# Block-summary rows ahead of the local rows, and a new order table, in an attention layer with two feed-forward layers

## The chip, the cores and the metric

The kernel runs on one core of a Trainium2 chip. The metric is the device time of one execution in microseconds (us). The core's engines are named as the profile names them: PE does matrix multiplications (PEld is the loading of their stationary operand), DVE and ACT work on rows of 128 partitions, POOL is a third such engine, SP issues the transfers between the memory outside the core (HBM) and its own (SBUF); 16 DMA engines carry them out. PE writes into PSUM. Each engine runs its instructions strictly in the order in which they were written, and waits where an operand is not there yet.

## What is computed

Two batches of 768 rows, eight heads of 64. Every row attends to the rows within 15 places of it, and to 24 summaries of the whole sequence: the maximum of k and the mean of v over each block of 32 rows. Its result, 1536 rows of 512 values, goes through two feed-forward layers 512 to 2048 to 512 with different gates. All of it is in float32.

```
k_sum = k.reshape(B, H, nb, block, D).max(axis=3)
v_sum = v.reshape(B, H, nb, block, D).mean(axis=3)
scores_l = scale * (q @ k.T), masked to |i - j| < 16
scores_s = scale * (q @ k_sum.T) + log(block)
a = softmax(concatenate([scores_l, scores_s]))
x = a @ concatenate([v, v_sum])
x = gate(x @ w_in) @ w_out         # h / (1 + exp(-1.702 h))
x = gate(x @ moe2_w_in) @ moe2_w_out  # h * cos(h)
```

## The kernel before

**Attention.** The 1536 rows are twelve units of 128. A unit is two halves (g) of 64 rows, and a half sees 96 local rows (`GW`) and the 24 summaries (`NB`), 120 columns in all (`GC`), the local ones first. Scores come out with rows on partitions and 120 columns free (L407); DVE adds the mask and takes the maximum in one instruction (L414); ACT takes the exponential and its sum (L421); DVE divides (L424 to L430); PE transposes (L456 for the early units, L522 for the others), ACT copies the result to SBUF (L466, L525), and PE multiplies it with the values (L436). There the 120 columns are partitions: the window of values in `vw` or `vy` has its 96 local rows on partitions 0 to 95 and the 24 summary rows on 96 to 119. The local rows are loaded from `vwin` (`load_v`, L330, one transfer of 96 rows of 4 KB); the summary rows are written by `put_vsum`, once by ACT from PSUM (L360) and three times by POOL (L358).

**The summaries.** `ksum_of` (L368) takes block maxima on DVE. `vsum_mm` (L381) gets the block means of v from six matmuls of a 0 or 1/32 selector, sliced out of the tile `blk` 120 columns wide, of which 24 hold something.

**The first four units** (batch 0) are done in eight early pieces, n = 0 to 7: four heads of one unit each, heads 0 to 3 of the four units first. Each piece is: scores on PE, L414 on DVE, four exponentials on ACT, sums and norm on DVE, transposes on PE, copy on ACT, values on PE, and then the feed-forward input `xh`: its rounded part on ACT (L494), the rest on DVE (L495). Feed-forward steps for the first 512 rows can start when the `xh` of a head group of all four units is there. The eight other units are done between feed-forward steps.

**Feed-forward.** Per layer and per 512 rows there are 16 steps; each has 12 matmuls of 128x512 for h (L704), the gate on ACT and DVE, and 12 for the output (L830): 96 steps, 2304 matmuls. The weights come in 32 transfers of 1 MB (`w_load`, L611: chunk 0, 1, 2, ...). A chunk is converted before use (`convert`): L623 on ACT ("scale"), L629 ("low") and L633 ("join") on DVE, then twice L650 on ACT (high part) and L654 on DVE (low part). Chunk 0 holds what the first two h steps need.

**What sets the order.** Nothing is issued as it is written. Every piece of work is an `Op` with an engine, a planned duration and its predecessors; `order_of` lays them out engine by engine in planned time, by the length of the way behind each plus a number from the table `BONUS`, and the instructions are then written in that order (L260 is the line of nearly all transfers, since `dma` records them). The planned durations and the table only decide the order. All loads go through one queue, SP's, and the first 17 are chained in one written order (`wanted`): kf, qf, mask, identity, blk, vf, the window v of unit 0, weight chunk 0, the windows of units 1 to 3, weight chunk 1.

Of the kernel before, what the change touches and what calls it, by code (L numbers as in the profile page):

```python
# [55 lines left out]
    "at": 15248.9, "early at": 4670.1, "early exp": -10174.0, "early load v": 7117.2, "early load w": -9997.1,  # L56
    "early norm": -26626.0, "early pv": -19642.9, "early s": -8955.9, "early sum": -21555.4, "early t": 28276.7,
    "early ttr": -8099.7, "early w hi": -32048.9, "early w join": 3108.9, "early w lo": -20901.2,
    "early w low": 14427.2, "early w scale": 2678.5, "early xc": 272.9, "early xl": -7387.2, "evac": 19328.8,
    "exp": -10511.6, "g hi": 6093.0, "g lo": 3352.9, "gate": 20097.5, "h": -2002.2, "ksum": -8099.2,  # L60
    "load blk": -15675.4, "load ident": -7247.9, "load k": 9987.0, "load k1": -2486.3, "load kf0": -3352.8,
    "load kf1": 4225.3, "load mask": 42433.3, "load q": -7043.4, "load qf0": -12789.8, "load qf1": -4538.6,
    "load v": -6728.3, "load vf": 10952.8, "load vf1": 226.0, "load w": -6499.3, "norm": 3592.2, "out": -2000.2,
    "put ksum": 23793.3, "put vsum": -23481.1, "put vsum pool": -2105.8, "pv": 1324.1, "pv s": -3914.3,
    "s": -10696.2, "store": -2998.8, "sum": -22560.9, "sum vf1": 1824.3, "t": 10815.7, "ttr": -15482.4,
    "vsb": 3823.5, "vsum": 12059.7, "vsum1": -840.6, "w hi": 5478.0, "w join": -4468.7, "w lo": -3558.6,
    "w low": 6921.0, "w scale": 7315.3, "x hi": -12587.8, "x lo": -7344.2, "xc": -4143.9,
# [108 lines left out]
def order_of(ops):  # L176
# [24 lines left out]
    start, end = listed(ops, START, before, behind, {o: way[o] + BONUS.get(o.kind, 0.0) for o in ops}, True)  # L201
# [8 lines left out]
def local_global_attention_two_ffn(  # L210
# [64 lines left out]
    vsb = ex[1][0:GC, 1024:1024 + DM]  # L275
    blk = ex[1][:, 1536:1800]
# [49 lines left out]
    d_blk = dma("load blk", 0.37, blk, blkc)  # L326
    d_id = dma("load ident", 0.2, ident, identc)

    def load_v(i, dst, *deps):
        return dma(("early " if i < UT else "") + "load v", 1.6, dst[0:GW].rearrange("p g d -> p (g d)"), vwin[i], *deps)  # L330

    def load_k(i, *deps):
        b, j = divmod(i, NTILE)

        def fn():
            for g in range(2):
                c = 128 * j + 64 * g
                nc.sync.dma_start(out=kw[:, :, g, 0:GW], in_=kT[b, :, :, c:c + GW].rearrange("h p s -> p h s"))

        return op("load k", "DMA", 2.2, fn, *deps)  # L340

    def load_q(i, *deps):
        b, j = divmod(i, NTILE)
        return dma("load q", 1.1, qw, qT[b, :, :, 128 * j:128 * j + 128].rearrange("h p s -> p h s"), *deps)

    def put_ksum(b, hf, *deps):
# [3 lines left out]
            lambda: nc.gpsimd.tensor_copy(out=kw[:, 2 * hf:2 * hf + 2, :, GW:GC], in_=src.to_broadcast([128, 2, 2, NB])), *deps  # L350
# [772 lines left out]
```

## Time and profile before

| | |
|---|---|
| median of 3 runs | 590.74 us (590.04 to 593.53) |
| span of the profiled execution | 590.6 us |
| PE busy | 579.7 us, 98% |
| DVE busy | 400.2 us, 68% |
| ACT busy | 296.0 us, 50% |
| POOL busy | 15.9 us, 3% |
| moved by DMA | 55.06 MB, 93 GB/s over the span |

A busy PE in this table is not a PE at its peak. Shares over the whole span also hide that the first 40 us are a stage of another kind than the rest, so the rows below are mostly from there.

### The profile page before, as it was taken

What the parts mean: (1) busy time and instruction counts of PE and PEld (TensorE: products, weight loads), DVE (VectorE), ACT (ScalarE), POOL (GpSimd) and SP (SyncE); (2) the same over time, 40 slices, a digit from 0 to 9 for tenths busy, and PEclk for the clock granted to TensorE, in tenths of its full rate; (3) what the DMA queues carried; (4) which work ended last, traced back from release to release, by engine and by line L of the source; (5) the groups of instructions that cost most, each with busy time, mean ns of one, the idle gap of its engine ahead of it and who ended that gap; (6) DMA issues with size and microseconds to landing.
All of it is one profiled execution on the core that took longest, in us unless ns stands there. A gap on an engine that the chain in (4) does not pass through costs nothing.

```text
span 590.6 us, 8597 instructions
## 1 busy us (share of the span) xinstructions
PE 579.7 (98%) x3319; PEld 474.8 (80%) x3319; DVE 400.2 (68%) x810; ACT 296.0 (50%) x607; POOL 15.9 (3%) x19
## 2 busy tenths in 40 slices
PE   7899999999999999999999999999999999999997
PEld 5478888888888888888888888888888888888886
DVE  5689998965242436578878866667666667765664
ACT  5688678855153344465667533335433334333333
POOL 0101400000000000000000000000000000000000
PEclk8899999999999999999999999999999999999999
DMA  9978867733021116145550000000100000100001
GB/s 313 268 237 294 304 205 249 245 107 108 1 72 33 39 28 214 61 154 181 188 202 0 2 1 1 0 1 0 72 1 1 0 2 0 72 0 2 0 1 71
DMA packets 24200, 55.06 MB, mean 93 GB/s; under 512 B 9824, under 2 KB 15072, under 8 KB 20064
## 3 DMA queue, kind: packets, MB, share of 16 engines
q1 hardware_dynamic: 24016, 54.39, 28.3%
q8 instruction: 26, 0.43, 0.3%
q14 instruction: 14, 0.11, 0.1%
q10 hardware_dynamic: 144, 0.13, 0.1%
HBM read 51.37 MB, written 3.15 MB: 92 GB/s over the span
## 4 chain that ended last, share of the span: by engine, by line
PE 94%; DMA 3%; ACT 1%; SPq 0%; issue 0%; DVE 0%; ACTq 0%
PE h_ps L704 45%; PE acc L830 44%; DMA raw<-in_w_dram 2%; PE x_ps L436 2%; PE s_ps L407 1%; PE t_ps L522 1%; DMA kf<-in_kT_dram 1%; SPq L260 0%; PE t_ps L456 0%; ACT at_early L466 0%; ACT ex L421 0%; ACT wc L623 0%; PE vs_ps L381 0%; ACT xh L494 0%; ACT w L650 0%
## 5 line engine op out<-in xcount | busy, mean ns | idle before, releaser
L704 PE MATMUL h_ps<-xh,w 128*128 128x512 f32 x1152 | 291.8, 391 | 0.0
L830 PE MATMUL acc<-g,w 128*128 128x512 f32 x1155 | 290.4, 390 | 0.0
L704 PEld LDWEIGHTS h_ps<-xh,w 128*128 128x128 f32 x1152 | 215.5, 188 | 45.5 <-issue 0.3
L830 PEld LDWEIGHTS acc<-g,w 128*128 128x128 f32 x1155 | 216.1, 188 | 44.7 <-issue 0.5
L760 ACT CAST g<-gt 128x512 fp32r<-128x512 f32 x96 | 59.7, 622 | 91.5 <-PE acc L830 83.1
L764 DVE TENSOR_TENSOR g<-gt,g 128x512 fp32r<-128x512 f32 x96 | 66.1, 690 | 41.2 <-ACT g L760 40.9
L752 ACT ACTIVATE gt<-gt,half_pi 128x512 f32<-128x512 f32 x48 | 34.7, 723 | 64.1 <-DVE gt L748 64.0
L732 DVE SCALAR_TENSOR_TENSOR gt<-gt,h_ps 128x512 f32<-128x512 f32 x48 | 32.8, 684 | 28.8 <-ACT gt L726 28.8
L756 DVE TENSOR_TENSOR gt<-gt,h_ps 128x512 f32<-128x512 f32 x48 | 33.0, 688 | 26.8 <-ACT gt L752 26.8
L633 DVE SCALAR_TENSOR_TENSOR wc<-wc,raw 128x1024 uint32<-128x1024 uint32 x32 | 41.2, 1289 | 12.7 <-ACT wc L623 12.6
L728 ACT ACTIVATE gt<-h_ps 128x512 f32<-128x512 f32 x48 | 28.6, 597 | 35.4 <-PE h_ps L704 35.4
L726 ACT ACTIVATE gt<-h_ps 128x512 f32<-128x512 f32 x48 | 28.5, 595 | 34.1 <-PE h_ps L704 33.8
L654 DVE TENSOR_TENSOR w<-wc,w 128x512 fp32r<-128x512 f32 x64 | 45.3, 716 | 0.0
L623 ACT ACTIVATE wc<-raw 128x1024 f32<-128x1024 f32 x32 | 36.8, 1150 | 12.3 <-DVE w L654 7.3
L650 ACT CAST w<-wc 128x512 fp32r<-128x512 f32 x64 | 38.4, 618 | 4.4 <-DVE wc L633 4.2
L736 DVE TENSOR_SCALAR gt<-gt 128x512 f32<-128x512 f32 x48 | 20.5, 426 | 29.6 <-ACT gt L728 29.5
L740 DVE SCALAR_TENSOR_TENSOR r<-gt,h_ps 128x512 f32<-128x512 f32 x48 | 33.4, 696 | 1.6
L744 DVE SCALAR_TENSOR_TENSOR gt<-gt,r 128x512 f32<-128x512 f32 x48 | 32.9, 686 | 1.4
L629 DVE TENSOR_SCALAR raw<-raw 128x1024 uint32<-128x1024 uint32 x32 | 22.7, 709 | 5.7 <-DMA raw<-in_w_dram 5.7
L748 DVE TENSOR_SCALAR gt<-gt 128x512 f32<-128x512 f32 x48 | 20.4, 424 | 0.9
L414 DVE CUSTOM_DVE_ANT_0 room<-s_ps,mask_sb 128x120 f32<-128x120 f32 x32 | 6.8, 279 | 15.2 <-PE s_ps L407 15.2
L421 ACT ACTIVATE ex<-ex 128x120 f32<-128x120 f32 x32 | 12.2, 383 | 6.3 <-DVE ex L414 6.3
(74 smaller groups left out, 289.3 us busy)
## 6 DMA issues: line engine op xcount, KB each, us to landing
raw<-in_w_dram SPq DMA_DIRECT2D x32, 1024.0 KB, 4.8
win<-in_vwin_dram SPq DMA_DIRECT2D x9, 384.0 KB, 5.3
win<-in_kT_dram SPq DMA_DIRECT2D x16, 192.0 KB, 4.5
out_dram<-xf SPq DMA_DIRECT2D x11, 256.0 KB, 2.0
win<-in_qT_dram SPq DMA_DIRECT2D x8, 256.0 KB, 5.5
kf<-in_kT_dram SPq DMA_DIRECT2D x4, 400.0 KB, 5.4
k<-in_kT_dram SPq DMA_DIRECT2D x4, 400.0 KB, 8.1
vf<-in_v_dram SPq DMA_DIRECT2D x3, 512.0 KB, 8.5
```

The source lines that it names most:

```text
L623: nc.scalar.activation(out=t.bitcast(FP32), in_=raws[m][:, :, 1].bitcast(FP32), func=ACTF.Prelu, scale=REBIAS, alpha=SIGN)
L633: nc.vector.scalar_tensor_tensor(out=t, in0=t, scalar=3, in1=raws[m][:, :, 0], op0=ALU.logical_shift_left, op1=ALU.bitwise_or)
L650: nc.scalar.copy(out=w[:, 0, :], in_=mids[m][:, 512 * a:512 * (a + 1)].bitcast(FP32))
L654: nc.vector.tensor_tensor(out=w[:, 1, :], in0=mids[m][:, 512 * a:512 * (a + 1)].bitcast(FP32), in1=w[:, 0, :].bitcast(FP32), op=ALU.subtract,)
L704: nc.tensor.matmul(out=hs[i], lhsT=w[:, a, c], rhs=x[:, b, :], start=(k == 0 and n == 0), stop=(k == KD - 1 and n == 2),)
L740: nc.vector.scalar_tensor_tensor(out=r, in0=gts[i], scalar=-C1, in1=hs[i], op0=ALU.mult, op1=ALU.add)
L744: nc.vector.scalar_tensor_tensor(out=gt, in0=gt, scalar=-C2, in1=rs[0], op0=ALU.mult, op1=ALU.add)
L752: nc.scalar.activation(out=gt, in_=gt, func=ACTF.Sin, bias=half_pi)
L756: nc.vector.tensor_tensor(out=gt, in0=gt, in1=hs[i], op=ALU.mult)
L760: nc.scalar.copy(out=g[:, 0, :], in_=gts[i])
L764: nc.vector.tensor_tensor(out=g[:, 1, :], in0=gts[i], in1=g[:, 0, :].bitcast(FP32), op=ALU.subtract)
L830: nc.tensor.matmul(out=accs[d][:, c], lhsT=w[:, a, 128 * d:128 * (d + 1)], rhs=g[:, b, c], start=(f == 0 and n == 0), stop=(f == NF - 1 an ...
```

## The change

The 120 columns of a unit change places: the 24 summaries come first, the 96 local rows behind them. In the free dimension (k windows, mask, scores) this is another slice of the same tile. In the partition dimension the value windows now have summaries on partitions 0 to 23 and local rows on 24 to 119. The selector slices of `blk` shrink from 120 to 24 columns, the tile from 264 to 68 columns, and the block means come out on partitions 0 to 23. The planned durations of most transfers are lowered, and the table `BONUS` gets other values and one more entry for many single operations (`"at#4"` is the fifth of its kind). `order_of` adds both.

```diff
 BONUS = {
-    "at": 15248.9, "early at": 4670.1, "early exp": -10174.0, "early load v": 7117.2, "early load w": -9997.1,
...
+    "at": -196105.0, "at#0": -6600.5, "at#1": 28.6, "at#10": 32.2, "at#12": -1.8, "at#13": -7258.6, "at#14": -4925.8,
...
-    start, end = listed(ops, START, before, behind, {o: way[o] + BONUS.get(o.kind, 0.0) for o in ops}, True)
+    made, urgency = {}, {}
+    for o in ops:
+        n = made[o.kind] = made.get(o.kind, -1) + 1
+        urgency[o] = way[o] + BONUS.get(o.kind, 0.0) + BONUS.get(f"{o.kind}#{n}", 0.0)
+    start, end = listed(ops, START, before, behind, urgency, True)
...
-    vsb = ex[1][0:GC, 1024:1024 + DM]
-    blk = ex[1][:, 1536:1800]
+    vsb = ex[1][0:NB, 1024:1024 + DM]
+    blk = ex[1][:, 1536:1604]
...
-        return dma(("early " if i < UT else "") + "load v", 1.6, dst[0:GW].rearrange("p g d -> p (g d)"), vwin[i], *deps)
+        return dma(("early " if i < UT else "") + "load v", 1.1, dst[NB:GC].rearrange("p g d -> p (g d)"), vwin[i], *deps)
...
-                nc.sync.dma_start(out=kw[:, :, g, 0:GW], in_=kT[b, :, :, c:c + GW].rearrange("h p s -> p h s"))
...
-        return op("load k", "DMA", 2.2, fn, *deps)
+                nc.sync.dma_start(out=kw[:, :, g, NB:GC], in_=kT[b, :, :, c:c + GW].rearrange("h p s -> p h s"))
...
+        return op("load k", "DMA", 1.8, fn, *deps)
...
-            src = (vw[GW:GC, 0, :] if eng == "POOL" else vs()[GW:GC, :]).rearrange("p (o c) -> p o c", o=1)
+            src = (vw[0:NB, 0, :] if eng == "POOL" else vs()[0:NB, :]).rearrange("p (o c) -> p o c", o=1)
...
-                nc.gpsimd.tensor_copy(out=dst[GW:GC], in_=src)
+                nc.gpsimd.tensor_copy(out=dst[0:NB], in_=src)
...
-                nc.scalar.copy(out=dst[GW:GC], in_=src)
+                nc.scalar.copy(out=dst[0:NB], in_=src)
...
-                    out=ps[0][0:GC, :], lhsT=sel, rhs=t, start=(a == 0), stop=(a == len(parts) - 1)
+                    out=ps[0][0:NB, :], lhsT=sel, rhs=t, start=(a == 0), stop=(a == len(parts) - 1)
...
-        o = op(("early " if m < 2 else "") + "load w", "DMA", 3.3, fn)
+        o = op(("early " if m < 2 else "") + "load w", "DMA", 2.65, fn)
...
-            mask[m, rows, 0:GW] = np.where(ok, 0.0, -8.0e9)[rows]
-            mask[m, rows, GW:] = 8.0 * np.log(float(BLK))
-    blk = np.zeros((128, 264), np.float32)
+            mask[m, rows, NB:] = np.where(ok, 0.0, -8.0e9)[rows]
+            mask[m, rows, 0:NB] = 8.0 * np.log(float(BLK))
+    blk = np.zeros((128, 68), np.float32)
```

What the table moves is seen in the written order of the engines. The first 15 transfers keep their order. Two places differ that matter for the text below; line numbers of the changed kernel are 71 higher there.

**ACT, early part, before.** `ex` holds the early pieces' probabilities (L421 is the exponential, four to a piece), `at_early<-t_ps` is the copy behind the transposes, `wc<-raw` the scale of a weight chunk, `win<-vs_ps` the copy of the block means, `xh<-x_ps` the feed-forward input. These rows follow the start-up of ACT:

```order
L421 ACTIVATE ex<-ex 128x120 x24
L466 COPY at_early<-t_ps 120x512 x2
L623 ACTIVATE wc<-raw 128x1024
L466 COPY at_early<-t_ps 120x512
L360 COPY win<-vs_ps 24x1024
L466 COPY at_early<-t_ps 120x512
L421 ACTIVATE ex<-ex 128x120 x4
L466 COPY at_early<-t_ps 120x512
L494 CAST xh<-x_ps 128x2x128 x3
L466 COPY at_early<-t_ps 120x512
L421 ACTIVATE ex<-ex 128x120 x4
L466 COPY at_early<-t_ps 120x512
```

**ACT, the same place in the change**, up to shortly ahead of the third scale (L694), in two pieces that follow each other; L721 (`w<-wc`) is the high part of a weight half:

```order
L492 ACTIVATE ex<-ex 128x120 x20
L537 COPY at_early<-t_ps 120x512
L492 ACTIVATE ex<-ex 128x120 x4
L694 ACTIVATE wc<-raw 128x1024
L537 COPY at_early<-t_ps 120x512
L492 ACTIVATE ex<-ex 128x120 x4
L537 COPY at_early<-t_ps 120x512
L431 COPY win<-vs_ps 24x1024
L537 COPY at_early<-t_ps 120x512
L694 ACTIVATE wc<-raw 128x1024
L565 CAST xh<-x_ps 128x2x128
```

and on:

```order
L537 COPY at_early<-t_ps 120x512
L492 ACTIVATE ex<-ex 128x120 x4
L565 CAST xh<-x_ps 128x2x128
L537 COPY at_early<-t_ps 120x512
L565 CAST xh<-x_ps 128x2x128
L721 CAST w<-wc 128x512
L537 COPY at_early<-t_ps 120x512
L721 CAST w<-wc 128x512
L565 CAST xh<-x_ps 128x2x128 x2
L721 CAST w<-wc 128x512
L565 CAST xh<-x_ps 128x2x128
```

Behind the last row come a copy, a cast of weights, the scale of chunk 2 and the last two casts to `xh`. What moved: the scale of chunk 0 stands behind 24 of the 32 exponentials in both. The scale of chunk 1 stood behind everything of the eight pieces but the last two casts to `xh`; it now stands ahead of all eight casts, the last four copies, the last piece's exponentials, and the high parts of chunk 0 as well.

**PE, start of the feed-forward part, before** (`x_ps<-at_early` are the values of a piece, 8 matmuls; `t_ps<-ident,ex` its transposes; `h_ps` is the first feed-forward product, `s_ps<-win` the scores of the fifth unit):

```order
L436 MATMUL x_ps<-at_early,win 64x64 x8
L436 MATMUL x_ps<-at_early,vy 64x64 x8
L456 MATMUL t_ps<-ident,ex 120x128 x4
L436 MATMUL x_ps<-at_early,vy 64x64 x16
L704 MATMUL h_ps<-xh,w 128x512 x24
L407 MATMUL s_ps<-win 64x120 x16
L704 MATMUL h_ps<-xh,w 128x512 x12
```

**PE, the same place in the change:**

```order
L507 MATMUL x_ps<-at_early,win 64x64 x8
L507 MATMUL x_ps<-at_early,vy 64x64 x8
L527 MATMUL t_ps<-ident,ex 120x128 x4
L775 MATMUL h_ps<-xh,w 128x512 x6
L507 MATMUL x_ps<-at_early,vy 64x64 x16
L775 MATMUL h_ps<-xh,w 128x512 x12
L478 MATMUL s_ps<-win 64x120 x16
L775 MATMUL h_ps<-xh,w 128x512 x21
```

What moved: the first six h matmuls now stand ahead of the last two pieces' values, of which six more stand behind these together with the first six that need them; before, all 24 stood behind them.

## Rows read from the trace of the kernel before

**Rows 1.** The page: its span, and the chain that ended last, by engine

```profile
span 590.6 us, 8597 instructions
PE 94%; DMA 3%; ACT 1%; SPq 0%; issue 0%; DVE 0%; ACTq 0%
```

**Rows 2.** The chain that ended last, in order of time: start, length, what

```profile
9.25 14.56 DMA raw<-in_w_dram
23.83 1.17 ACT wc L623
...
37.06 5.67 PE h_ps L704 x24
42.73 0.98 PE s_ps L407 x32
...
69.39 1.13 PE x_ps L436 x32
...
79.89 0.87 PE t_ps L522 x8
...
320.87 2.72 PE acc L830 x12
...
575.87 10.92 PE acc L830 x51
```

**Rows 3.** Busy time of the engines in single stretches, last column DMA

```profile
core 0: us, PE busy (x) PEld busy (x) DVE busy (x) ACT busy (x) POOL busy (x), PEclk, DMA share, GB/s
10.60:13.00 2.40, 1.75 (x49) 1.66 (x44) 2.40 (x17) 2.40 (x14) 0.27 (x1) 0.50 1.05 403
15.50:18.00 2.50, 2.50 (x9) 1.27 (x8) 2.40 (x17) 2.47 (x13) 0.00 (x0) 0.86 1.04 229
21.00:23.50 2.50, 1.81 (x37) 0.94 (x35) 0.00 (x0) 0.00 (x0) 0.00 (x0) 1.00 1.01 231
47.00:49.00 2.00, 2.00 (x10) 1.68 (x9) 2.00 (x10) 2.00 (x9) 0.00 (x0) 1.00 1.09 242
...
60.00:80.00 20.00, 20.00 (x149) 16.48 (x148) 19.16 (x41) 14.50 (x34) 6.53 (x4) 1.00 0.91 298
```

**Rows 4.** Time line of SP's queue: issue of qf's last part, and of chunk 1

```profile
5.25 0.43 SPq L260 DMA_DIRECT2D qf<-in_qT_dram  x1
...
13.32 0.35 SPq L611 DMA_DIRECT2D raw<-in_w_dram  x1
```

**Rows 5.** DMA issues from 0 to 14 us: count, KB each, us to landing

```profile
vf<-in_v_dram SPq DMA_DIRECT2D x3, 512.0 KB, 8.5
vy<-in_vwin_dram SPq DMA_DIRECT2D x3, 384.0 KB, 16.6
...
qf<-in_qT_dram SPq DMA_DIRECT2D x1, 512.0 KB, 6.7
```

**Rows 6.** The same from 13 to 14 us: chunk 1 alone

```profile
raw<-in_w_dram SPq DMA_DIRECT2D x1, 1024.0 KB, 18.1
```

**Rows 7.** Time line of ACT: start, us, line, what, [idle before]

```profile
23.83 1.17 ACT L623 ACTIVATE wc<-raw 128x1024 f32<-128x1024 f32 x1 [3.27 <-DMA raw<-in_w_dram]
...
31.84 0.40 ACT L421 ACTIVATE ex<-ex 128x120 f32<-128x120 f32 x1
...
33.37 0.57 ACT L466 COPY at_early<-t_ps 120x512 f32<-120x512 f32 x1
33.83 0.92 ACT L494 CAST xh<-x_ps 128x256 fp32r<-128x256 f32 x3
...
37.20 0.67 ACT L494 CAST xh<-x_ps 128x256 fp32r<-128x256 f32 x2
37.71 1.21 ACT L623 ACTIVATE wc<-raw 128x1024 f32<-128x1024 f32 x1
38.80 1.15 ACT L650 CAST w<-wc 128x512 fp32r<-128x512 f32 x2
```

More of the change, by code (lines that the diff above doesn't have):

```diff
@@ L55 @@
 BONUS = {
-    "at": 15248.9, "early at": 4670.1, "early exp": -10174.0, "early load v": 7117.2, "early load w": -9997.1,
[L57 to L65, printed above, removed]
@@ L66 @@
-    "vsb": 3823.5, "vsum": 12059.7, "vsum1": -840.6, "w hi": 5478.0, "w join": -4468.7, "w lo": -3558.6,
-    "w low": 6921.0, "w scale": 7315.3, "x hi": -12587.8, "x lo": -7344.2, "xc": -4143.9,
[4 rows of a table added]
+    "early exp": -65767.3, "early exp#0": 661.0, "early exp#1": -7530.0, "early exp#2": 28137.7,
+    "early exp#3": -14656.7, "early exp#4": 4650.2, "early exp#6": -30830.4, "early exp#7": -626.6,
+    "early load v": 214345.9, "early load v#0": -15680.8, "early load v#1": 2.4, "early load v#2": 518.7,
@@ new lines @@
+    "early load v#3": 12867.0, "early load w": -411934.4, "early load w#0": 321.9, "early load w#1": 14057.4,
+    "early norm": -306696.0, "early norm#0": 15760.2, "early norm#2": -14594.3, "early norm#3": -2569.6,
[4 rows of a table added]
+    "early sum": 275382.8, "early sum#1": -23.3, "early sum#2": 4177.6, "early sum#3": -10598.2,
+    "early sum#5": -12838.7, "early sum#7": -12517.5, "early t": 118180.7, "early t#0": 33421.6, "early t#2": 25.0,
+    "early t#3": -9628.9, "early t#4": 23978.7, "early t#5": 4867.2, "early t#7": -8240.3, "early ttr": 587321.8,
[9 rows of a table added]
@@ new lines @@
+    "early xl#4": -30099.0, "early xl#5": -2412.6, "early xl#6": 9860.3, "early xl#7": -23090.7, "evac": 304508.4,
[9 rows of a table added]
+    "ksum#4": 2193.7, "ksum#5": 7253.2, "ksum#6": -110.7, "load blk": 336165.2, "load ident": 188140.6,
[4 rows of a table added]
+    "load mask": 42989.5, "load mask#0": 10036.8, "load q": -478923.9, "load q#0": -265.7, "load q#1": -1.4,
[10 rows of a table added]
+    "put ksum#0": -12867.5, "put ksum#1": 8968.0, "put ksum#2": 9522.4, "put ksum#3": -7170.0, "put vsum": -662672.0,
+    "put vsum pool": 679063.3, "put vsum pool#0": 399.1, "put vsum pool#1": 39184.6, "put vsum#0": 13821.5,
[26 rows of a table added]
@@ L302, in local_global_attention_two_ffn @@
     for hp in range(H // 2):
-        o = dma("load k1", 1.14, k1[hp], kT[1, hp])
+        o = dma("load k1", 0.95, k1[hp], kT[1, hp])
         d_k1.append(ring["w0"].take(o, True))
-    d_mask = dma("load mask", 0.6, mask_sb, maskc)
+    d_mask = dma("load mask", 0.53, mask_sb, maskc)
     d_vf = [[], []]
@@ L309, in local_global_attention_two_ffn @@
     for a, t in enumerate(vf[0]):
-        d_vf[0].append(ring["w1"].take(dma("load vf", 1.4, t, r[a]), True))
+        d_vf[0].append(ring["w1"].take(dma("load vf", 1.36, t, r[a]), True))
     r = v[1].rearrange("(p t a) d -> t p a d", t=S // (2 * GW), a=2)
     for a, t in enumerate(vf[1]):
-        d_vf[1].append(ring["w1"].take(dma("load vf1", 1.5, t, r[a]), True))
+        d_vf[1].append(ring["w1"].take(dma("load vf1", 1.3, t, r[a]), True))
     row = lambda n: vf[1][n // 2][:, n % 2, :]
@@ L325, in local_global_attention_two_ffn @@
         ring["w1"].take(boot(), True)
-    d_blk = dma("load blk", 0.37, blk, blkc)
+    d_blk = dma("load blk", 0.2, blk, blkc)
     d_id = dma("load ident", 0.2, ident, identc)
     def load_v(i, dst, *deps):
-        return dma(("early " if i < UT else "") + "load v", 1.6, dst[0:GW].rearrange("p g d -> p (g d)"), vwin[i], *deps)
+        return dma(("early " if i < UT else "") + "load v", 1.1, dst[NB:GC].rearrange("p g d -> p (g d)"), vwin[i], *deps)
     def load_k(i, *deps):
@@ L390, in vsum0 @@
     def vsum0(tag):
-        return vsum_mm(0, tag, [(blk[:, 20 - 4 * a:20 - 4 * a + GC], vf[0][a // 2][:, a % 2, :], a // 2, d_vf[0][a // 2])
+        return vsum_mm(0, tag, [(blk[:, 20 - 4 * a:20 - 4 * a + NB], vf[0][a // 2][:, a % 2, :], a // 2, d_vf[0][a // 2])
                                 for a in range(S // 128)])
     def vsum1(tag):
-        return vsum_mm(1, tag, [(blk[0:GW, 140:140 + GC], row(0), 3, ready[0])])
+        return vsum_mm(1, tag, [(blk[0:GW, 44:44 + NB], row(0), 3, ready[0])])
     def edge(i):
@@ L984, in after_pv @@
             vs1, vm1 = vsum1("h")
-            vs1_done = ring["h"].use(op("vsb", "ACT", 0.5, lambda: nc.scalar.copy(out=vsb, in_=vs1()[0:GC]), vm1))
+            vs1_done = ring["h"].use(op("vsb", "ACT", 0.5, lambda: nc.scalar.copy(out=vsb, in_=vs1()[0:NB]), vm1))
             pvv = put_vsum("ACT", lambda: vsb, vw, pv, vs1_done)
```

16 lines of the change are left out of this document (8 added, 8 removed), and 65 rows, old and new, of the table BONUS.

## The prediction, made before the changed kernel was run

> **What bounds the kernel now.** I read the chain that ended last first. PE is 94% of it [rows 1], and in its pieces PE works without a break from 37.06 us on to 575.87 + 10.92 = 586.8 us [rows 2]. A feed-forward matmul takes 2.72 / 12 = 0.227 us there. Take 43.71 us as the mark, where the first 24 h matmuls and the fifth unit's scores are done (42.73 + 0.98) [rows 2]. Behind it lie 2304 - 24 matmuls, 516.9 us, and of the eight later units eight times values at 1.13, seven times scores at 0.98 and eight times transposes at 0.87 us, 22.9 us [rows 2], and one block-mean matmul, about 1 us. That is 540.8 of the 543.1 us up to 586.8: **all waits of PE behind the mark are worth 2.3 us at most**, and the last 3.8 us are copies and stores that the change leaves alone. So the time is the mark plus 547, and what can be won is nearly all ahead of the mark.
>
> There the kernel waits for its loads. The stretches [rows 3] show DMA fully busy (share 1.01 to 1.05) but at two rates: 403 GB/s from 10.6 to 13.0 us, 229 and 231 GB/s at 15.5 to 18 and 21 to 23.5 us. The slow ones are those in which the 96-row windows of v move (the loads land in the order of issue); a later stretch, 47 to 49 us, in which only such 96-row loads move, has 242. In the stretch from 21 us DVE and ACT do nothing at all: weight chunk 0, issued at 9.25, lands 14.56 us later, at 23.8 us, and ACT's scale, which had stood 3.27 us, starts with it [rows 2, 7]. Chunk 1 was issued at 13.32 and took 18.1 us, to 31.4 us [rows 4, 6].
>
> **The change, part by part.**
>
> *The selector.* The six block-mean matmuls still stream 512 columns; a narrower stationary operand saves loading, in a stretch where PE has idle time (1.81 of 2.50 us busy, [rows 3]): nothing. If PE had no slack there, it would be some tenths. `blk` is 98 KB smaller: at 403 GB/s 0.25 us off every later landing.
>
> *The free dimension* (k windows, mask, early scores): same sizes, same counts, nothing. Likewise the copies of the summaries: the same 24 partitions' worth on ACT and POOL.
>
> *The value windows on partitions 24 to 119.* Same bytes, same 96 rows, same 4 KB packets, another place. No row shows a load to that place, so I bound it. From the landing of qf at 5.25 + 6.7 = 11.95 us [rows 4, 5] to chunk 1's at 31.4 us come three loads of 512, four of 384 and two of 1024 KB [rows 5, 6], 5.24 MB in 19.5 us, 269 GB/s. At the slow end the place changes nothing and chunk 1 lands at 31.4 - 0.25 = 31.2 us. At the fast end everything moves at 403 GB/s: 13.0 us, chunk 1 at 24.7 us and, by the same reckoning for the 3.01 MB up to it, chunk 0 at 19.2. I take 26.5 us for chunk 1, three quarters of the way to the fast end. The reason to lean there: the slow rate belongs to loads that all sit on partitions 0 to 95, loads over all 128 partitions beside no such load reach 403, and what the new place evens out is the halves: 64 of the 96 rows lay in the lower 64 partitions and 32 in the upper, now it is 40 and 56. The reason not to go all the way is that the number of rows stays 96.
>
> One rule speaks against this. By the Trainium skill, page "SBUF — State Buffer", section on the DMA port swizzle, a partition's port follows from bits of its number, and partitions 32 apart share one. Counted with it, 0 to 95 puts eight rows on eight of the ports and four on the others, and 24 to 119 does the same with other ports: the fullest port is as full as before. By the rule's 27.2 GB/s for a port that would be 1.2 us for a window, an estimate, and unchanged; the sum would be that of the first rival. The trace has a window at 393 KB / 231 GB/s = 1.7 us, so the port count alone does not explain the slow rate either.
>
> *The order of ACT.* Chunk 1's scale now stands ahead of the work that the first h matmuls need, so ACT's path to them starts at chunk 1's landing. Behind it, up to the last cast to `xh`: two scales (chunks 1 and 2) at 38.80 - 37.71 = 1.09, four exponentials 33.37 - 31.84 = 1.53, four copies at 33.83 - 33.37 = 0.46, eight casts to `xh` at (37.71 - 37.20) / 2 = 0.26, four casts of weights at 1.15 / 2 = 0.58 us [rows 7]: 2.18 + 1.53 + 1.84 + 2.08 + 2.30 = 9.9 us. From 26.5 us that is 36.4; with the end of the last cast and its rest on DVE, as long as a cast each, 37.0 us. Chunk 2's load waits for chunk 0's join, which is past by then; behind chunk 1 it needs 1 MB and some small loads, some 5 us, so it is there when its scale comes at 26.5 + 8.3.
>
> *The order of PE.* Twelve of the first 24 h matmuls need no late cast, and stand ahead of those that do; they fit before 37.0. From there PE needs six h, the scores and six h to be at the mark: 1.36 + 0.98 + 1.36 = 3.7 us, so the mark is at 40.7 us instead of 43.7.
>
> **Sum:** 590.6 - 3.0 = **587.6 us**, against the profiled execution's own 590.6, which is the median of the runs (590.74) to 0.1 us.
>
> **Rivals.**
>
> 1. *The windows land as slowly as before* (by the port count above). Then the new order is worse than the old one: ACT stands idle at chunk 1's scale until 31.2 us with the exponentials of the last piece, four copies and eight casts behind it, which before were done while chunk 1 was on its way. 31.2 + 9.9 + 0.6 + 3.7 = 45.4 us for the mark, 1.7 later: **592.3 us**. It turns to a loss as soon as chunk 1 lands later than 29.5 us. For it: 96 rows stay 96 rows. Against it: the two rates above.
> 2. *All loads reach the full rate.* Chunk 1 at 24.7: mark at 38.9, **585.8 us**. If PE's 2.3 us of waits behind the mark went too, 583.5.
> 3. *The clock of PE.* It was granted at 0.50, the lower of the two levels (1.2 GHz), at 10.6 to 13.0 us, where PE was busy 1.75 of 2.40 us, and at 1.00 at 21 to 23.5 [rows 3]. The early pieces are spread thinner in the new order. If the clock is low when the h matmuls start, the 3.7 us up to the mark double: **591.3 us** at worst. Against it: before, it was high at that point.
> 4. *The gain is given back behind the mark.* DVE is busy 19.16 of 20 us at 60 to 80 us [rows 3]; PE can only run 3 us ahead if DVE does. If it doesn't, PE waits: **590.6 us**. Against it: in the new order DVE takes up the wait it had at 21 us, and has the first two instructions of chunk 3 done ahead of where it had them.
>
> **How the numbers follow.** Forecast (chunk 1 at 25.5 to 28) 0.45; rival 1, 0.20; rival 2, 0.15; rival 3, 0.08; rival 4, 0.12. The likeliest gives 587.6 us. The range goes from 584.6 (rival 2 with half of PE's waits gone too) to 592.6 (rival 1); its own range for the forecast is 586.6 to 589.1. About 1%, 5.9 us, is what a measurement of this kernel can tell from no change. Faster by over 1% (below 584.8) needs rival 2 and nearly half of PE's waits: 0.08. Slower by over 1% (above 596.6) needs rival 1 and rival 3 together and more: 0.04. Within 1%: 0.88.
>
> **What would show it.** Right: the stretches with windows of v at clearly over 300 GB/s; chunk 0 there by about 21 us and chunk 1 by 26 to 28; ACT's second scale starting with that landing, with little idle time ahead; 24 h matmuls and the scores done near 40.7 us; the rest of PE without gaps. Wrong: 230 to 240 GB/s as before and ACT idle for over 2 us at the second scale (rival 1); a granted clock under 1.00 between 30 and 45 us (rival 3); PE waiting for DVE's low parts of weights between 45 and 230 us (rival 4).

## The result, and the profile after

| | before | after |
|---|---|---|
| median of 4 runs each, side by side | 591.69 us (590.04 to 593.53) | 596.6 us (595.12 to 597.13) |
| ratio, 95% interval | | 1.008, 1.0053 to 1.0107 |
| span of the profiled execution | 590.6 us | 594.4 us |

The change made the kernel slower by 0.8%. That is within 1%, where the forecast had put it, but on the other side: it had said 587.6 us, and 592.6 at most. The medians differ by 4.9 us, the two profiled executions by 3.8. In the runs on record the time is some 1.8 us longer than the span, so the profiled execution of before was 0.7 us slower than its median and that of after 0.4 us faster; the account that follows is of the 3.8. The chain that ended last was 94% PE in [rows 1]; now it reads:

```profile
span 594.4 us, 8588 instructions
PE 88%; DMA 6%; DVE 4%; ACT 1%; issue 0%; SPq 0%; ACTq 0%
```

DMA has gone from 3% to 6%, and DVE from 0% to 4%. The stretches with the windows of v, which answer to [rows 3] (last three columns: granted clock, DMA share, GB/s):

```profile
core 0: us, PE busy (x) PEld busy (x) DVE busy (x) ACT busy (x) POOL busy (x), PEclk, DMA share, GB/s
...
15.50:18.00 2.50, 2.50 (x50) 1.45 (x46) 2.47 (x14) 1.65 (x8) 0.00 (x0) 0.91 1.04 259
20.50:23.50 3.00, 1.30 (x4) 0.10 (x1) 0.00 (x0) 0.00 (x0) 0.00 (x0) 1.00 1.05 223
...
60.00:80.00 20.00, 19.65 (x141) 15.68 (x140) 19.38 (x44) 14.72 (x34) 0.53 (x2) 1.00 0.80 263
```

The new place did not make the loads fast: 259 and 223 GB/s, where 229 and 231 stood, and where the forecast asked for over 300. From 20.5 to 23.5 us DVE and ACT do nothing, as before, and PE is busy for 1.30 of 3.00 us, against 1.81 of 2.50. The time line of ACT shows what it waited for (answers to [rows 7]):

```profile
24.25 1.16 ACT L694 ACTIVATE wc<-raw 128x1024 f32<-128x1024 f32 x1 [5.18 <-DMA raw<-in_w_dram]
25.30 0.57 ACT L537 COPY at_early<-t_ps 120x512 f32<-120x512 f32 x1
...
31.50 1.17 ACT L694 ACTIVATE wc<-raw 128x1024 f32<-128x1024 f32 x1 [0.49 <-DMA raw<-in_w_dram]
...
40.88 0.66 ACT L565 CAST xh<-x_ps 128x256 fp32r<-128x256 f32 x2
```

Chunk 0's scale starts at 24.25 us, after 5.18 us of idle time instead of 3.27; the second copy of transposes, which was done ahead of it before, stands behind it. Chunk 1's scale starts when chunk 1 lands, 31.4 us. PE, whose next transposes need the room that the second copy frees, stands for 4.13 us (time line of PE):

```profile
25.93 0.89 PE L527 MATMUL t_ps<-ident,ex 128*120 128x128 f32 x4 [4.13 <-ACT at_early L537]
```

And it gets to the mark late (chain that ended last, start, length, what; answers to [rows 2]):

```profile
12.95 18.47 DMA raw<-in_w_dram
...
35.19 0.49 ACT at_early L537
...
35.72 0.65 PE t_ps L527 x4
36.38 1.60 PE x_ps L507 x48
37.97 0.58 PE t_ps L527 x4
38.55 1.39 PE h_ps L775 x6
39.95 1.13 PE x_ps L507 x32
41.08 2.99 PE h_ps L775 x12
44.06 0.98 PE s_ps L478 x32
45.04 1.62 PE h_ps L775 x6
...
67.86 5.72 DMA raw<-in_w_dram
...
79.78 0.62 PE t_ps L593 x4
```

The mark, 43.71 us before, is at 45.04 + 1.62 = 46.66 us: 2.95 us later. On this chain ACT is the limit only up to 35.68 us; from 35.72 us on PE works without a break to the mark, for 10.94 us. Before, PE's unbroken run up to the mark began a little later, at 36.33 us, with the row

```profile
36.33 0.73 PE x_ps L436 x16
```

and the 24 h matmuls and scores of [rows 2] behind it, 7.38 us in all. PE starts 0.61 us earlier than before and has 3.56 us more to do, mostly 64 value matmuls and eight transposes (as the chain counts them) that were done ahead of that point before: that is the 2.95.

The other 0.85 us of the 3.8 come behind the mark, most of them by 90 us, on a chain through DVE that ends in a weight chunk landing at 73.6 us and in the transposes of the sixth unit at 79.78.

What fills ACT up to the last cast to `xh` is seen by grouping its instructions by line from chunk 0's scale on, in the kernel after (24.2 to 41.35 us) and, in the second fence, before (23.8 to 37.65 us); "x" is the count, the end of the row the idle time ahead:

```profile
L537 ACT COPY at_early<-t_ps 120x512 f32<-120x512 f32 x7 | 4.1, 584 | 0.7 <-PE t_ps L527 0.7
L694 ACT ACTIVATE wc<-raw 128x1024 f32<-128x1024 f32 x3 | 3.6, 1188 | 5.7 <-DMA raw<-in_w_dram 5.7
...
L721 ACT CAST w<-wc 128x512 fp32r<-128x512 f32 x4 | 2.6, 638 | 0.0
...
```

```profile
L466 ACT COPY at_early<-t_ps 120x512 f32<-120x512 f32 x6 | 3.5, 586 | 1.1 <-PE t_ps L456 1.0
...
L623 ACT ACTIVATE wc<-raw 128x1024 f32<-128x1024 f32 x2 | 2.4, 1184 | 3.3 <-DMA raw<-in_w_dram 3.3
...
L650 ACT CAST w<-wc 128x512 fp32r<-128x512 f32 x2 | 1.2, 644 | 0.0
...
```

The exponentials and the casts to `xh` are the same eight each. The new order puts one copy, one scale and two casts of weights more between chunk 0 and the last cast to `xh`: 0.46 + 1.09 + 1.15 = 2.7 us by the prices of [rows 7]. Measured from the start of chunk 0's scale to the end of the last cast, ACT took 41.54 - 24.25 = 17.3 us, against 37.87 - 23.83 = 14.0 before; 1.0 us of the difference is more idle time. So the new order has more work on ACT here, but the casts at its end are not what the mark waited for: PE came to the six h matmuls that need them at about 42.6 us, and they were ready at 42.07.

### The profile page after: what moved, and what is told of

Same layout as the page of the kernel before. It is cut to its first block, busy times and chain, and to the rows that moved or that the text cites. A ratio compares the mean times of both kernels' runs of the same rounds, so it can differ in the third digit from the quotient of the medians.

```text
span 594.4 us, 8588 instructions
## 1 busy us (share of the span) xinstructions
PE 581.3 (98%) x3319; PEld 471.2 (79%) x3319; DVE 399.8 (67%) x810; ACT 295.7 (50%) x607; POOL 15.3 (3%) x19
## 4 chain that ended last, share of the span: by engine, by line
PE 88%; DMA 6%; DVE 4%; ACT 1%; issue 0%; SPq 0%; ACTq 0%
PE h_ps L775 42%; PE acc L901 41%; DMA raw<-in_w_dram 4%; PE x_ps L507 2%; PE s_ps L478 1%; PE t_ps L593 1%; DMA vf<-in_v_dram 1%; DVE w L725 1%; DMA kf<-in_kT_dram 1%; DVE wc L704 1%; ACT sm_main L492 0%; DVE raw L700 0%; DVE g L835 0%; DVE gt L803 0%; DVE sm_main L485 0%
## 5 line engine op out<-in xcount | busy, mean ns | idle before, releaser
L775 PE MATMUL h_ps<-xh,w 128*128 128x512 f32 x1152 | 280.1, 391 | 0.0
L901 PE MATMUL acc<-g,w 128*128 128x512 f32 x1155 | 278.5, 389 | 0.0
L835 DVE TENSOR_TENSOR g<-gt,g 128x512 fp32r<-128x512 f32 x96 | 66.1, 689 | 28.2 <-ACT g L831 26.6
L807 DVE TENSOR_SCALAR gt<-gt 128x512 f32<-128x512 f32 x48 | 20.5, 426 | 41.3 <-ACT gt L799 41.2
L721 ACT CAST w<-wc 128x512 fp32r<-128x512 f32 x64 | 38.8, 620 | 13.0 <-PE acc L901 9.5
L694 ACT ACTIVATE wc<-raw 128x1024 f32<-128x1024 f32 x32 | 37.1, 1159 | 14.7 <-DMA raw<-in_w_dram 10.8
L704 DVE SCALAR_TENSOR_TENSOR wc<-wc,raw 128x1024 uint32<-128x1024 uint32 x32 | 39.0, 1221 | 5.6 <-ACT wc L694 5.5
L819 DVE TENSOR_SCALAR gt<-gt 128x512 f32<-128x512 f32 x48 | 20.5, 426 | 1.4
L750 DVE TENSOR_TENSOR xh<-xf,xh 128x512 fp32r<-128x512 f32 x20 | 13.1, 686 | 0.5 <-PE h_ps L775 0.5
```

What stands on the lines that cost most here:

```text
L694: nc.scalar.activation(out=t.bitcast(FP32), in_=raws[m][:, :, 1].bitcast(FP32), func=ACTF.Prelu, scale=REBIAS, alpha=SIGN)
L704: nc.vector.scalar_tensor_tensor(out=t, in0=t, scalar=3, in1=raws[m][:, :, 0], op0=ALU.logical_shift_left, op1=ALU.bitwise_or)
L721: nc.scalar.copy(out=w[:, 0, :], in_=mids[m][:, 512 * a:512 * (a + 1)].bitcast(FP32))
L775: nc.tensor.matmul(out=hs[i], lhsT=w[:, a, c], rhs=x[:, b, :], start=(k == 0 and n == 0), stop=(k == KD - 1 and n == 2),)
L835: nc.vector.tensor_tensor(out=g[:, 1, :], in0=gts[i], in1=g[:, 0, :].bitcast(FP32), op=ALU.subtract)
L901: nc.tensor.matmul(out=accs[d][:, c], lhsT=w[:, a, 128 * d:128 * (d + 1)], rhs=g[:, b, c], start=(f == 0 and n == 0), stop=(f == NF - 1 an ...
```

## The experiments

Each run has a run of the kernel before on the same chip beside it; ratios are to that.

**1. The loads alone.** Series of transfers, each series queued behind the one before:

```diff
+    for k in range(4):
+        d(out=buf[0:96, k], in_=row4[96 * k:96 * k + 96])
+    close(0)
+    for k in range(4):
+        d(out=buf[24:120, k], in_=row4[96 * k:96 * k + 96])
...
```

> Leaves out the whole computation: only series of loads from HBM into one tile, each series started when the one before has landed, so that nothing else moves beside it. Four transfers a series unless said. In the order of the lines: 96 rows of 4 KB on partitions 0 to 95 (L36), on 24 to 119 (L39), on 32 to 127 (L42), 128 rows of 4 KB (L45), 128 rows of 3 KB (L48), 96 rows of 8 KB (L51, two), 96 rows of 4 KB from a source in which they stand 8 KB apart (L54), eight of 64 rows (L57), eight of 32 rows (L60), 112 rows (L63), eight of 48 rows on 0 to 47 and 48 to 95 in turn (L66), 64 and 32 rows in turn (L69), three times 32 rows (L72), and the windows of v themselves (L75). Theory of the forecast (the place counts: halves of the partitions unevenly filled): L36 about 235 GB/s, L39 and L42 clearly more, 300 and up. Rival A (the place does not count, the number of rows does): L36, L39, L42 alike within 5%, near 235, and 128 rows at some 400; 64 and 32 rows then tell which numbers are slow. Rival B (packets of 4 KB are slow whatever the rows): 128 rows of 4 KB as slow as 96, and 96 rows of 8 KB near 400. Rival C (the windows are slow only beside other loads, or from their own source): L36 near 400 and L75 alone slow, or none slow.

The first loads of a series are issued while the last of the one before are on their way, so the rates are taken in stretches inside the series. Measured in one execution, for L36, L39, L42, L45, L48, L51, L54, L57, L60, L63 and L75, in this order (last column GB/s):

```profile
14.00:18.00 4.00, 0.46 (x3) 0.00 (x0) 1.00 1.04 262
20.50:24.00 3.50, 0.39 (x3) 0.00 (x0) 1.00 1.04 266
26.50:29.50 3.00, 0.47 (x3) 0.00 (x0) 1.00 1.06 276
32.00:34.80 2.80, 0.31 (x2) 0.00 (x0) 1.00 1.02 408
36.50:38.80 2.30, 0.77 (x5) 0.00 (x0) 1.00 1.03 402
41.00:45.50 4.50, 0.31 (x2) 0.00 (x0) 1.00 0.99 254
49.00:52.00 3.00, 0.32 (x2) 0.00 (x0) 1.00 1.01 292
54.50:62.00 7.50, 0.84 (x6) 0.00 (x0) 1.00 1.05 206
64.00:67.50 3.50, 0.80 (x5) 0.00 (x0) 1.00 1.06 204
70.50:75.00 4.50, 0.32 (x2) 0.00 (x0) 1.00 1.05 256
...
98.00:100.50 2.50, 0.16 (x2) 0.00 (x0) 1.00 1.02 279
```

96 rows move at 262, 266 and 276 GB/s at partitions 0, 24 and 32: the place is worth at most 5%, less than what separates loads at one place: the windows of v (279) and 96 rows that stand 8 KB apart in HBM (292) lay on partitions 0 to 95, as the 262 did. 128 rows move at 408 and 402, with packets of 4 and of 3 KB; 96 rows with packets of 8 KB at 254, 112 rows at 256, 64 and 32 rows at 206 and 204. Rival A holds: it is the number of rows, and in this series only the full 128 are fast. 96 rows cut into 64 and 32, into twice 48 or three times 32 came to 242, 214 and 244. The forecast's idea of uneven halves of the partitions is refuted.

By the Trainium skill, page "SBUF — State Buffer", section on the DMA port swizzle, 32 and 64 partitions reach the same eight ports of 27.2 GB/s each, an estimate of 218 GB/s; the trace agrees, with 204 and 206. By the same count the fullest port has eight rows of a transfer of 96 or 112, an estimate of 327 and 381 GB/s: the trace has 262 and 256, so the count does not carry that far. The same page of the Trainium skill, in its section "Can I just issue two DMAs to hit both halves?", says: "The only way to hit all 16 ports is one transfer spanning all 128 partitions." That only such transfers had the full rate agrees with it, while the ports themselves no run here shows.

**2. The new place with the old order, and the new order with the old place.** Kernel place_only takes the table and the planned durations of before; kernel plan_only takes the old layout.

```diff
-    "at": -196105.0, "at#0": -6600.5, "at#1": 28.6, "at#10": 32.2, "at#12": -1.8, "at#13": -7258.6, "at#14": -4925.8,
...
+    "at": 15248.9, "early at": 4670.1, "early exp": -10174.0, "early load v": 7117.2, "early load w": -9997.1,
...
```

```diff
-    blk = ex[1][:, 1536:1604]
+    blk = ex[1][:, 1536:1800]
...
-                nc.scalar.copy(out=dst[0:NB], in_=src)
+                nc.scalar.copy(out=dst[GW:GC], in_=src)
...
```

> The new places of the summaries and of the local rows, the small selector and its small tile, with the table and the planned durations of before, so that the order of all engines is that of before. Theory (windows load no faster at partitions 24 to 119, the whole loss is the new order): as before within 0.1%, some 0.25 us less at most, chunk 1 landing at 31.2 to 31.5 us, the mark (first 24 h matmuls and the fifth unit's scores done) at 43.5 to 43.8 us. Rival (the new place itself costs time, or the loads are slower there): 2 to 6 us more than before.

> The layout of before (local rows first, on partitions 0 to 95, selector of 120 columns) with the planned durations and the table of the change, so that the order of all engines is that of the change. Theory (the order alone is the cause): as the changed kernel, 1.008 of before, mark at 46.4 to 47.0 us, the same further loss of about 0.9 us between 59 and 90 us. Rival (order and place act together: the order pays only with the loads at the new place, or loses only with them): off the changed kernel by over 1.5 us, to either side.

Measured: place_only 1.0022 (1.0002 to 1.0041, 593.28 us, 10 runs of 591.2 to 595.6), plan_only 1.0064 (1.0045 to 1.0083, 595.74 us), the changed kernel's 1.008 within its interval. In plan_only's chain the scores are done at 45.36 us and the six h behind them take 1.61, so the mark is at 47.0 us, and 0.8 us more are lost between 60 and 90 us, as in the changed kernel. So the order makes the loss, and the layout hardly any. Place_only was to be as before within 0.1%; its interval lies just clear of 1, and why is open. Its profiled execution, one of its two shortest (589.5 us span), does not show it: chunk 0 landed at 23.5 us and the mark was at 41.26 + 1.05 = 42.3, earlier than before. In the profiled executions of the kernels with 96-row windows, in which the 19 loads up to chunk 1 are chained in the same order, chunk 0 landed anywhere from 22.6 us (move12) to 25.5 us (after_then_before).

**3. Scales taken back.** Kernel move01: in the new order, the scale of chunk 0 goes behind the second copy and the copy of block means, and that of chunk 1 behind the last copy. Kernel move012 takes back chunk 3's scale too; move12 is move012 with chunk 0's scale left where the change put it.

```diff
+ MOVES = [
+     (('early w scale', 'ACT', 0), ('put vsum', 'ACT', 0)),
+     (('early w scale', 'ACT', 1), ('early at', 'ACT', 7)),
...
+     (('w scale', 'ACT', 1), ('g hi', 'ACT', 0)),
...
+ ]
- for o in order_of(ops):
+ for o in moved(order_of(ops), MOVES):
```

> The changed kernel, with two places of its order taken back and nothing else. The scale of chunk 0 on ACT goes behind the second copy of transposes and the copy of the block means (its two parts on DVE behind the seventh norm); chunk 1's scale on ACT goes behind the last copy of transposes, with the high parts of chunk 1 and chunk 2's scale behind the last cast to xh, and their parts on DVE likewise. Theory (the loss ahead of the mark is those two conversions standing ahead of the early pieces while their chunks have not landed): mark at 39 to 41 us, time 586 to 588 us, 3 to 5 less than before. Rival (the order behind the mark is poor in itself, or DVE, which takes chunk 1's parts later, holds PE behind the mark): mark early, but the time at 590 to 594 us.

> The kernel move01 (scales of chunks 0 and 1 taken back behind the work that needs none of them), with the scale of chunk 3 as well behind the first two gates, and its parts on DVE and the casts of its halves behind it, as in the kernel before. In move01 the mark came at 41.1 us, and PE then stood 4.25 us, since ACT waited 3.06 us for chunk 3 ahead of the first gate. Theory (the whole loss is scales that stand ahead of work while their chunk is on its way): no stop of PE behind the mark, time 1 to 3 us under before, 0.995 to 0.998. Rival (with the scales moved back DVE, which carries the later parts, holds PE): mark near 41, a wait of PE for DVE of 2 us or more behind it, time at or over that of before.

> As the kernel move012, but the scale of chunk 0 stays where the change put it, ahead of ACT's second copy of transposes. It tells what that one place costs. Theory (PE's 4.13 us at the second copy come from this place, and about half of them reach the mark): mark 1.5 to 3 us later than in move012, time 589.5 to 592.5. Rival (the place of chunk 0's scale costs nothing, since chunk 1 lands at 31.4 anyway): mark and time as move012 within 0.6 us.

Measured: move01 1.0095 (1.0072 to 1.0118), move012 1.0086 (1.0062 to 1.011), move12 1.0124 (1.01 to 1.0148). In move01 the mark came at 41.1 us (39 to 41 was expected), 2.6 ahead of before, with windows as slow as ever. Then PE stood (rows of PE's and of ACT's time line in move01):

```profile
39.48 1.66 PE L807 MATMUL h_ps<-xh,w 128*128 128x512 f32 x6
45.38 5.29 PE L807 MATMUL h_ps<-xh,w 128*128 128x512 f32 x15 [4.25 <-DVE gt L835]
```

```profile
41.93 1.16 ACT L726 ACTIVATE wc<-raw 128x1024 f32<-128x1024 f32 x1 [3.06 <-DMA raw<-in_w_dram]
```

ACT waits for chunk 3 ahead of the first gate, and the whole gain is gone. Move012 puts that scale behind the gate; then the same happens one chunk on: ACT waits 1.92 us for the next chunk at 53.87, the transposes of the fifth unit wait 2.3 us, and by 65 us the kernel is some 5 us behind before in the work that PE has left. The theory that a few early scales are the whole loss is refuted: taking one back only hands its wait to a later chunk. Chunk 0's place (move12 against move012) costs some 2 us by the medians, 599.15 against 596.97; move12's mark at 42.4 us was no later than move012's at 42.9, but in its execution chunk 0 had landed 1.8 us earlier (22.57 against 24.40 us), so these profiles do not tell where the 2 us go.

**4. Half of one order and half of the other.** `FIRST` lists the work up to the mark in the other kernel's order, and `begun` puts it ahead of the rest.

```diff
-        for o in order_of(ops):
+        for o in begun(ops, order_of(ops), FIRST):
```

> The new layout, 96-row windows, and an order put together from the two: everything that the change has planned up to the mark (the first 24 h matmuls and the scores of the fifth unit, 155 pieces of work) in the order of the change, all that comes behind in the order of before. Theory (two separate losses: some 3 us ahead of the mark, 0.9 us behind it): mark at 46.4 to 47.0 us, and the lag behind before stays at 2.7 to 3.2 us to the end, ratio 1.0045 to 1.006. Rival (one loss only: what the change's order gains or loses behind the mark follows from its early part): the lag grows to 3.6 us or more, ratio 1.007 and up.

> The counterpart: new layout, 96-row windows, the 152 pieces of work up to the mark in the order of before, all behind in the order of the change. Theory of two separate losses: mark at 42.5 to 43.8 us, the lag behind before 0.8 to 1.0 us from 90 us on, ratio 1.001 to 1.002. Rival (the change's order behind the mark converts chunk 3 and the next ahead of the gates, for which their loads, let go by the conversions of chunk 1, come too late with the early part of before, as in the kernels move01 and move012): PE stands 3 us or more within 20 us behind the mark, ratio 1.005 and up.

Measured: after_then_before 1.0113 (1.0085 to 1.0141), before_then_after 1.0104 (1.0057 to 1.0151). Neither mixture is faster than the new order whole (1.008, 1.0053 to 1.0107), and both are slower than two separate losses would be: that theory is refuted. In before_then_after the early part runs as before (scores done at 43.4 us), and then the rival's wait comes:

```profile
46.54 5.24 PE L810 MATMUL h_ps<-xh,w 128*128 128x512 f32 x15 [3.11 <-DVE gt L838]
```

```profile
43.37 1.17 ACT L729 ACTIVATE wc<-raw 128x1024 f32<-128x1024 f32 x1 [1.13 <-DMA raw<-in_w_dram]
```

The two parts of an order are tied by the loads: chunk 3 can be fetched only when chunk 1 is converted, and in all four traces its load is issued 0.03 us behind the end of chunk 1's join. The changed kernel converts chunk 1 early and issues chunk 3's load at 34.59 us; before_then_after issues it at 38.53, before at 38.80, and move01 at 36.68. The late part of the change counts on the early one. After_then_before is 4.7 us behind before at the mark; its chunks landed 1.3 us later than in the changed kernel (scales at 25.51 and 32.80 us), and why is open. It loses 1.9 us more between 58 and 66 us, 1.1 of them in waits of PE for DVE.

**5. The loads made fast.** What the change was planned for can be had with 128 rows: the windows of the first four units are loaded with padding, and the summaries are written over it afterwards. Kernel new128 does this in the new order, old128 in the old order and layout, place128 in the old order and the new layout.

```diff
+        c = slice(0, 128) if i < UT else slice(NB, GC)
...
+    for x, y in zip(vput, d_v):
+        x.deps.append((y,))
```

> The changed kernel with its order, but the windows of v of the first four units are loaded as 128 rows of 4 KB: the 24 rows ahead of the local ones and the 8 behind them are zeros in HBM, and the copies of the summaries write over the 24 afterwards (each copy now waits for its window's load, which is long past). 128 rows moved at 403 GB/s in the series of loads, 96 rows at 235 to 265. By the steps of the forecast: chunk 0 at 19.5 to 21 us, chunk 1 at about 26.0 us (5.77 MB at 403 GB/s from 11.95 us, 0.25 less for the small selector), ACT's second scale without a wait of its own. Theory (the order is good where the loads are there, and lost only because they were not): mark at 40 to 42 us instead of 46.7, time 2 to 4 us under before, 0.993 to 0.997. Rival (the order is worse in itself, wherever the loads are): chunk 1 by 26.5 and still a time at or over that of before.

> The kernel before with its order and its layout, with the windows of v of the first four units loaded as 128 rows, the local rows first. Same bytes as in the kernel new128. Theory (ACT's 3.27 us at the scale of chunk 0 is the stage's limit, and the loads alone end it): chunk 0 at 20 to 21 us, the chain up to the first h matmul 2.5 to 3.3 us earlier, mark at 40.5 to 41.5 us, time 2 to 3 us under before, 0.994 to 0.997; the rival to the new order: as good as it with the same loads. Rival (something else sets the end of that stage, such as the block means and their copy): chunk 0 early, but the mark within 1 us of 43.7.

> The new layout (summaries first, selector of 24 columns, small tile) in the order of before, with the windows of v of the first four units as 128 rows. It is the kernel old128 with the new places. Theory (the places and the selector are worth nothing): mark at 39 to 40 us, ratio within 0.001 of old128's 0.9947. Rival (the new layout costs some 1 us, as the ratio 1.0022 of the kernel place_only would have it): 0.9955 to 0.998, and the trace shows where, by a granted clock of 0.50 in stretches where old128 has 1.00 or by a wait of PE that old128 has not.

Measured: new128 1.0029 (1.0016 to 1.0043, 593.86 us), old128 0.9947 (0.9927 to 0.9967, 588.54 us), place128 0.9949 (0.9928 to 0.9971, 588.61 us). The loads did what was expected: in old128, from 10.6, 15.5 and 21 us on,

```profile
10.60:13.00 2.40, 0.89 (x34) 0.85 (x34) 2.40 (x18) 2.40 (x15) 0.27 (x1) 1.00 1.05 392
15.50:18.00 2.50, 2.48 (x9) 0.99 (x7) 2.40 (x17) 2.48 (x13) 0.00 (x0) 1.00 1.05 424
21.00:23.50 2.50, 1.90 (x69) 1.62 (x68) 1.98 (x7) 2.45 (x4) 0.10 (x1) 1.00 1.07 429
```

and its chain, with chunk 0 at 20.56 us and the mark at 38.58 + 0.98 = 39.56 (40.5 to 41.5 was expected):

```profile
9.10 11.46 DMA raw<-in_w_dram
...
38.58 0.98 PE s_ps L408 x32
```

So 4.15 us are won at the mark in that execution and kept to the end. With the same loads the new order has chunk 0 at 20.3 us and chunk 1 at 26.6 us, the landing that the forecast assumed, and its mark is not at 40.7: it is at 42.91 + 6 x 0.227 = 44.3 us, or at 44.5 if the six take the 1.62 us that they took in the changed kernel. Its scales and last casts on ACT, PE from 30 to 36 us, and the chain there:

```profile
20.35 1.19 ACT L695 ACTIVATE wc<-raw 128x1024 f32<-128x1024 f32 x1 [0.88 <-DMA raw<-in_w_dram]
...
26.73 1.17 ACT L695 ACTIVATE wc<-raw 128x1024 f32<-128x1024 f32 x1 [1.10 <-DMA raw<-in_w_dram]
...
38.53 0.84 ACT L566 CAST xh<-x_ps 128x256 fp32r<-128x256 f32 x2 [0.39 <-PE x_ps L508]
```

```profile
30.00:36.00 6.00, 5.06 (x58) 4.60 (x58) 4.94 (x13) 4.33 (x13) 0.00 (x0) 0.51 0.74 243
```

```profile
30.95 1.11 PE t_ps L528 x4
32.05 2.81 PE x_ps L508 x48
34.87 1.04 PE t_ps L528 x4
35.91 1.93 PE h_ps L776 x6
```

The last casts to `xh` end at 39.37, 2.7 us later than 26.73 + 9.9; 2.05 of these are waits of ACT for PE (0.46, 0.48, 0.72 and 0.39), whose clock was granted at 0.51 from 30 to 36 us, after it had stood 1.70 and 0.94 us for ACT's copies. Old128 has 1.00 in all of this. The theory that the order is good where the loads are there is refuted, its rival holds. The chains tell how much of the 4.7 us or more between the two marks is the clock: the four rows above are 6.9 us, the same four pieces of work in the changed kernel, at a clock of 1.00, 4.2. So 2.7 us go with the clock, an estimate from these rows, and some 2 us are left for the order. The ten runs of new128 point the same way: the two with a mean clock of 0.996 and 0.997 took 591.8 and 592.8 us, the eight with 0.988 to 0.993 took 593.1 to 594.5; even the shortest is 2.6 us over the longest run of old128. Place128 shows no cost of the layout that these runs could tell; its mark was at 39.14 + 1.05 = 40.2 us.

**6. Chunk 0 ahead of the first window**, in old128:

```diff
+ MOVES = [(('early load v', 'DMA', 0), ('early load w', 'DMA', 0))]
```

> The kernel old128 with one transfer moved: the window of v of unit 0 (512 KB) stands behind weight chunk 0 in the queue, not ahead of it. In old128 chunk 0 landed at 20.56 us, ACT had waited 1.14 us for it, and the window of unit 0 was not read before 23.57 us. Theory (ACT from the landing of chunk 0 on sets the mark): chunk 0 earlier by 512 KB at 400 GB/s, 1.3 us, at 19.3 us; ACT's wait of 1.14 us gone; mark 0.7 to 1.1 us earlier than 39.5 us; ratio 0.9928 to 0.9937. Rival (another wait takes its place at once, the block means on PE, or the window, now landing last but for chunk 1): mark within 0.3 us of 39.5, ratio as old128, 0.9947.

Measured: 0.9949 (0.9936 to 0.9963), as old128. Chunk 0 landed at 8.55 + 10.7 = 19.3 us, as expected. ACT no longer waits for it, but 1.57 us for transposes on PE ahead of it; the scale starts at 20.91 us, and the mark is at 39.9. The rival holds: another wait took its place. Whether PE alone set it is not shown, since its granted clock from 15.5 to 18 us was 0.63 in this execution and 1.00 in that of old128.

**The kernel that beats both is old128** (place128 equals it): the order and the layout of before, with the first four windows as 128 rows, 3.3 us (0.5%) faster. Its runs and those of place128 and old128s, 15 in all, lie between 587.9 and 589.7 us, while those of before, side by side with them, range from 589.9 to 593.7.

## Why the prediction was wrong

*What bounds the kernel*: right for the order of before and for that of the change, each taken whole. From the mark to the end the forecast had 547 us; the changed kernel has 594.4 - 46.66 = 547.7, old128 586.4 - 39.56 = 546.8. But the 2.3 us of waits say what PE could win behind the mark, not what another order can lose there: move01 has 596.1 - 41.1 = 555.0, before_then_after 595.9 - 43.4 = 552.5. That "the time is the mark plus 547" holds for an order whose parts fit together, and only rival 4 allowed for one whose parts do not. That the profiled 590.6 was the median of the runs "to 0.1 us" is a slip: 590.6 is a span, and the times of the runs are some 1.8 us longer than their spans. It moves no term, since the gain was worked out as a difference.

*The step that failed first: chunk 1 at 26.5 us*, "three quarters of the way to the fast end". It landed at 31.4, the slow end (31.2). The reason given there, uneven halves, was an argument with no row behind it, and experiment 1 refutes it; the reason on the other side, "the number of rows stays 96", was the true one. The rows of before could not tell the two apart: every slow load had 96 rows and lay on partitions 0 to 95, every fast one had 128. With nothing in those rows to choose by, 0.45 went to one reading and 0.20 to the other, which happened.

*The order of ACT*: right in size for this landing, but not the path to the mark. 31.50 + 9.9 = 41.4, and the last casts ended at 41.54; the chain, though, left ACT at 35.68 us, and PE was the limit from there. With the early landing the size fails too: experiment 5 has 12.6 us from the second scale to the end of the last casts (39.37 - 26.73), for the sum of durations left out waits of ACT for PE, 2.05 us of them.

*The order of PE*, the second step that failed: mis-sized. After the last casts' rest on DVE, which ended at 41.31 + 0.76 = 42.07 us, there were to be six h, the scores and six h, 3.7 us; it took 46.66 - 42.07 = 4.6. "They fit before 37.0", ahead of the last casts, is the sentence that failed: PE had 10.94 us of work from 35.72 us on, and six of the twelve h stood behind the last 32 values in it, so that they were not done ahead. The last six took 1.62 us, not 1.36. So an early chunk 1 alone would not have given the 40.7 us: new128, where it came at 26.6 us, had its mark at 44.3 or later.

*The place of chunk 0's scale* was named in the change ("behind 24 of the 32 exponentials in both") and not costed: that the second copy had moved behind it was in the rows of the order, and gave PE 4.13 us of waiting at 25.93 us.

*Rival 1* was right in mechanism and side, and 1.3 us short at the mark (45.4 against 46.66): 0.9 by that PE term, most of the rest since chunk 1's scale started at 31.50, not 31.2. The sum also left out 0.85 us behind the mark, near rival 4's place (DVE busy 19.38 of 20 us at 60 to 80 us, PE 19.65). *Rival 3* did not happen here: the clock was 1.00 from 30 to 45 us. It had been 0.55 and 0.60 from 26 to 30 us, behind the 4.13 us for which PE had stood; ACT's waits for PE there, 0.82 and 0.73 us, were over before chunk 1 landed. Rival 3 did happen in new128.

*The selector, the free dimension, the place of the summaries as nothing*: right as far as place128 against old128 tells (0.9949 and 0.9947); place_only's 1.0022 stays open.

## What to carry to other kernels

Before a load is forecast to become faster, look in the trace for what the slow loads share and the fast ones do not. Here they shared two things, the row count and the place, and only a series of bare loads that changed one at a time told them apart. It was the row count: padding 96 rows to 128 moved a third more bytes in less time (512 KB at 408 GB/s are 1.3 us, 384 KB at 262 are 1.5), and let go the transfers beside it. An order on paper is worth only what its assumed landings are worth, and its parts are tied together by buffers that loads wait for: moving one conversion, or joining the start of one order to the end of another, handed the wait on to the next chunk. On every engine of a stretch, count the work between the last landing and the result in both orders, not on one alone: ACT had 2.7 us more by its prices, but the chain ended on PE, which had 3.56 us more.

## What was not expected of the hardware

In the series, 64 rows move no faster than 32 (206 and 204 GB/s), and 112 rows (256) no faster than 96 (262), while 128 have 408. Windows of 96 rows also slow what moves together with them: in the changed kernel windows and weight chunks are under way from 20.5 to 23.5 us with all 16 engines busy (share 1.05), and the sum is 223 GB/s; with windows of 128 rows old128 has 429 from 21 to 23.5 us.

The granted clock of the first 40 us differs between executions of the same early order: from 10.6 to 13.0 us it was 0.50 (the level of 1.2 GHz) in before, and 1.00 in old128 and place_only, which have the same early order on PE; in the 2.6 us ahead of it PE had been busy 2.33 us in before and 2.32 in old128, at a clock of 0.76 and 1.00. Whether this is why the times of before scatter over 4.2 us (44 runs) and those of old128 over 1.0 (4 runs) is not shown: the ten slowest of these runs of before have a mean clock of 0.990 to 0.994, the ten fastest one of 0.991 to 0.999.
